# Loading x's second pair of tiles ahead of w_mod in an adaLN attention and gMLP kernel

## The chip, the cores and the metric

The kernel runs on one NeuronCore of a Trainium2 chip. The metric is device time in microseconds (us) of one execution, as the median of several runs. The core has five engines with one instruction list each: PE (matmul), ACT, DVE, POOL and SP; SP here only issues DMAs. An engine works through its list in order and stops at an instruction whose semaphores are not there yet.

## The reference, cut to what matters

The input is one sequence of 2048 positions with 448 channels; all arrays are bfloat16.

```python
mod = (silu(c) @ w_mod).reshape(1, 6, 1, 448)     # c: (1, 448), w_mod: (448, 6 * 448)
sa, ca, ga, sb, cb, gb = (mod[:, i] for i in range(6))
h = layernorm(x) * (1 + ca) + sa
x = x + ga * A(h)       # qkv, 16 heads of 28, causal window of 256, softmax, wo
h = layernorm(x) * (1 + cb) + sb
x = x + gb * B(h)       # gelu(h @ w_in), halves z1, z2; (z1 * (w_sp @ layernorm(z2) + b_sp)) @ w_out
```

## The kernel before, in words

Positions are cut into 16 tiles of 128, channels into 4 groups of 112 (CP) on the partitions. The work goes through these stages, which overlap.

**Head.** c is loaded as one row (L397) and turned onto partitions by four products with a one-element `one` (L520), each with a filler product beside it; silu writes sc_sb (L524). w_mod's first two of six parts (shift and scale) are loaded into wmodA in four pieces (L415), by part and by half of the contraction, on SP and ACT. t_mA (L548 to L555) multiplies wmodA's columns, 112 at a time, with silu(c); the moving operand is one column of sc_sb repeated 112 times, so that the result lies on partitions. DVE copies it to modT (L579, L580). x's first four tiles come in two pairs: load_x0(0) first, load_x0(1) behind w_mod and half of wk (L413 to L421). Layer norm statistics run on DVE (L632, L635, L637) with a power on POOL (L639), the normalization writes xn (L650 on DVE, or L655 and L657). The first four tiles are turned by PE (L746) and modulated while they are copied out of PSUM (L755 on ACT, L757 on DVE) into hT. Later tiles are turned by SP's transposing DMAs (L467) and modulated in hT (L736, L738).

wk and wq land in wq_st and are copied with padding into WQK (L621, L622). K (L827), Q (L803 for the first four tiles, L769 for the others) and V (L847) are then projected tile by tile and copied out of PSUM to KT, qT and Vaug (L839, L840, L808, L809, L778, L779, L851, L852). QBD holds copies of qT's parts (L797, L822 and others). Fillers are products of a constant tile with itself (`busy`, L517), which give PE work while it has none.

**Attention.** For each of 16 tiles and two halves of the heads: scores (L932, L962, L973), exponential on ACT (L918), causal and window mask on DVE (L981, L1002), product with V (L1009), division (L1023, L1025), a transposing DMA of o_sb, the product with wo (L1035) and the addition to x (L1039), the second layer norm and its transposing DMA. gg_sb (L601) holds the gates ga and gb, with which POOL scales wo (L605) and w_out (L1051).

**gMLP.** z1 and z2 (L1150, L1129) with gelu on ACT, the product with w_sp (L1174), z1 times it (L1178, L1181), w_out (L1193), addition to x (L1203), stores (L1208). w_sp is loaded by transposing DMAs on SP.

**What sets the order.** Every piece of work is an `Op` with the engines that could run it and an estimate of its duration. The string PLAN lists all ops, one word each: the engine's letter (p, a, d, t for POOL, s), the op's number, and the PSUM bank or buffer that it takes. It was searched ahead of time against the estimates, with `prio`, `land` (when a load is due) and `after` (an order between ops) as its guides, and is fixed in the file. `Sched.order` deals the words out to the engines' lists, `Sched.waits` finds the semaphore waits, `Sched.emit` writes the instructions. So PLAN alone decides on which engine a movable op runs, and where in that engine's list.

Of the kernel before, what the change touches and what calls it, by code (L numbers as in the profile page):

```python
# [5 lines left out]
BF16 = mybir.dt.bfloat16  # L6
# [6 lines left out]
d24 d22 p50.3 p52.1 p55.0 p46.1 p57.0 p54.3 a0 a3 d23 p37.0.1 p71.0 p63.3 p69.1 p73.0 p74.1 p61.0 p62.3 p60.2 s1  # L13
s2 d108 d110 s4 s6 s10 s8 s12 a5 a7 a9 a38 a39 p75.1 t27 t28 t29 t32 t33 t30 t31 a100 a106 d111 d109 t112 t113
t26 p42.1 p43 p58.3 p48.1 p44.0 p45 d114.3 d115.1 p124.6 p77.2 p64.0 p51.3 d83 p127.0 p70.1 p66.0 p72.2 p67.3
p65.0 p78.1 d82 d125 d128 t101 p139.1 t25 t102 p56.0 d126 p81.3 p76.1 p47.0 p80.3 p59.2 p53.1 p49.2 a105 t103
d129 p140 a141 a40 p148.5 p149 a150 d116 d118 d117 d119 d176 d180 d182 d178 d177 d183 d181 d179 t104 t107
p145.6 p146 a147 p136.1 p137 a138 s11 p151.5 p152 a153 p79.2 t120 t121 d123.0 d122.1 p130.7 p133.0 a134 d41
d131 t184 t185 d186.3 p68.0 p372.0 a373.2 p142.6 p143 a144 d132 d135 p154.7 p170.1 p171 p155 p378.0 s13 d241
d247 d245 s14 d308 d242 d156 d246 s15 s193 t187 t188.1 s194 p163.0 p164 t189 t190.2 s195 t191 t192.0 s196  # L20
a379.4 p397.0 t34 t35 d248 t36 d243 d382 d312 d306 d380 d309 d374 d376 p173.6 a172 p157.1 p158 p160.7 p174
a398.1 a165 p90.0 p91 d92 a399 p404.0 d402 d310 d244 d400 d169 p161 p93.0 t85 t84 a175 a159 p86.1 p87 d88 d89
p375.0 p377 p94 a405.3 a406 p425.0 p381 p383 a197 d199 t200 d198 p210.1 p211 t249 t250 t252 t253.2 t254 d95
p217.0 p218 s16 s19 a426.0.0 p433.0 d384 d385.1 p401.0 s386 a166 d407 p403 p408 a212 p204.1 p205 d311 d219
p201.0 p202 d409 s259 t255.1 d307 d313 t314 d167 d168 s260 d251.0 t256 s258 t257.3 s261 t315 t321 t319 t99 t98
t96 t97 a434.2 p453.0 d429 d203 d436 a206 p207.1 p208 p410 d411 d209 d430 d412.2 s413 d435 a162 p427.0 p220.0
p221 a454.1.1 p461.0 p229.1 p230 d457 a428 a222 p226.0 p227 d228 p431.0 p432 a462.6 p481.0 d463 a231 a482.4.2
s852 s17 s18 p437 p438 d439 d215 d440.1 s441 p223.0 p224 a225 p232.1 d458 d216 d213 d464 p489.0 a490.2 d492
p233 p235.0 p236 a237 p459.0 p455.0 p508.0 p414.0 p415 d416 t262 t264 t263 t265 a234 p387.1 p388 d389 d486
a456 p460 p465 p466 d467 d468.0 d485 t320.1 s325 t322.2 s469 s326 s21 a214 p483.0 p272.0 p273 a509.0.0 p536.0  # L30
p269.1 p270 d491 p487.0 a484 p510.0 p488 p493 a537.5.1 p516.0 d274 d316.0 s323 t317 t318.3 p494 d390 d391 t392
t393 d512 d513 d495 d496.1 s497 d394.1 t395 s324 t330 t327 t329 a271 a511 p266.1 p267 p538.0 p275.0 p276
a517.6 d519 d518 d417 p564.0 a268 p442.1 a277 p282.0 p443 p514.0 d444 d281 p515 p283 a565.4.2 d569 p544.0 d418
d445 t419 d278 p291.1 p520 p521 d522 d446 d540 d447 d541 a539 p292 a284 p288.0 p289 t448 t449 s396 t450.0 t328
t451 s20 s848 d523.1 s524 a545.2 p572.0 d546 d547 d568 a293 p294.1 p295 a290 p238.0 p239 p542.0 p543 p548
a573.0 d574 p592.0 p549 d550 d551.0 s552 s846 a240 p470.0 p471 p566.0 a296 p285.1 p286 d472 d279 a593.3.0
p600.0 p300.0 d575 d473 d596 d280 p570.0 p301 d302 a567 p571 p576 a601.2 p619.0 d602 p577 d597 d578 d579.1
s580 a287 p525.1 p337.0 p338 d474 p526 d527 a620.4.1 p627.0 d624 d623 d603 p594.0 a339 p553.0 p554 d555 p340.1
p598.0 p341 a628.5 p647.0 d475 d630 a595 p599 p604 d556 p605 d606 d607.0 s608 s452 t476 t477 t478.2 t420 t421
t422.1 d557 t423 t479 s480 s424 t558 t559 t560 a342 p498.1 p499 p621.0 d500 p297.0 p298 a648.6.2 p675.0 d629  # L40
d651 a622 p649.0 p625.0 p331.1 p332 a299 p334.0 p626 a676.3.0 p655.0 d501 d502 t503 d333 d652 d528 d679 p631
p632 p335 d633 d336 d344 a650 p347.1 p677.0 p348 a656.4 d657 p683.0 a678 a349 p609.0 p610 d611 d658 d680
d634.2 s635 a684.5 p359.1 p360 a361 p350.0 p351 a352 d612 d343 d613 d346 d345 p703.0 a704.2.1 d707 t504 d505.0
d686 t561.1 t562 t822 t614 t615 p353.1 p354 a355 p303.0 p304 a305 p653.0 p711.0 p654 p659 p660 d661 d662.1
s663 p356.1 p705.0 p581.0 p582 a712.1 p730.0 d685 d583 d713 d708 p681.0 p682 p687 p688 d689 d690.2 d714 a706
a731.0.2 d735 d734 p732.0 a733 t821 s563 s691 s853 s847 t506 s507 d529 t530 p357 d358 p738.0 a739.5 p365.0
p709.0 p710 p715 p366 a367 p716 d717 d584 d718.1 s719 t531 t532 t533.1 d585 t586 t824 t823 t534 t587 t588
t589.2 d740 d741 p758.0 a759.1.1 d763 p760.0 p362.0 p363 a364 a761 p664.1 p665 d666 d762 p736.0 p766.0 a767.3
# [12 lines left out]
t915 p945 a953 d955 d973 d954 d972 d941 d948 d949 d956 t950 d974 d896 t951 t957 t958 a836 a835 p1038.0 p1039.1
# [191 lines left out]
def bass_adaLN_cond__sliding_block__mixer_gmlp__prompt_kernel(  # L253
# [257 lines left out]


    hC = Hold(bM)
    hCW = Hold(bL)

    def busy(h):
        return lambda e: e.matmul(  # L517
# [57 lines left out]
    for op in fillers[30:]:  # L575
        op.deps.update(t_mA)
# [699 lines left out]
```

## Time and profile before

| what | us |
|---|---|
| median of 3 runs | 277.72 |
| the 3 runs | 277.67 to 277.77 |
| the profiled execution | 277.95 |
| its span, first to last instruction | 276.2 |
| busy in the span: PE, PEld (weight loads) | 268.6, 154.3 |
| busy in the span: DVE, ACT, POOL | 163.6, 124.1, 132.3 |

Between the first and the last instruction lies the span; the time of an execution is some 1.75 us longer. A busy engine in this profile is one with an instruction in flight, and the ends of matmuls are modelled. Idle time is put down to the instruction whose semaphore came last. Line numbers (L827) are those of the kernel before; in the changed file most stand one to four lines earlier (L1174 is L1173 there, L827 is L826).

### The profile page before, as it was taken

The numbers are of one execution on the slowest core, as the hardware profiler recorded it, in microseconds if no ns is written. First come the engines' busy times: TensorE is split into PE (matmuls) and PEld (weight loads), VectorE is DVE, ScalarE is ACT, GpSimd is POOL, SyncE is SP. The second block draws the span as 40 slices with busy tenths as digits, with TensorE's granted clock in tenths as the row PEclk, the third lists the DMA queues.
The fourth block names the chain that finished last, engine by engine and source line by source line (L and its number), as shares of the span: only waits on it lengthen the run. The fifth ranks groups of instructions, "written<-read, shape, count | busy, mean of one in ns | idle before, by whom it ended". The sixth has DMA issues, their size and how long they took to land.

```text
span 276.2 us, 8436 instructions
## 1 busy us (share of the span) xinstructions
PE 268.6 (97%) x3745; PEld 154.3 (56%) x3755; DVE 163.6 (59%) x365; ACT 124.1 (45%) x146; POOL 132.3 (48%) x190
## 2 busy tenths in 40 slices
PE   8989999999999999999999999999999999999995
PEld 5966677687667766454444444444444444445452
DVE  3599999999998999968979310014302213121454
ACT  3489899998889887365885500000000000000000
POOL 7563899438086285667567003316643303241400
PEclk9999999999999999999999999999999999999999
DMA  7999448578232497578599996000000001000114
GB/s 204 263 309 183 80 82 194 101 70 135 38 62 40 44 136 167 105 117 134 115 173 156 209 187 119 0 1 0 2 0 0 17 2 33 0 0 2 33 50 133
DMA packets 67302, 25.55 MB, mean 92 GB/s; under 512 B 58497, under 2 KB 66178, under 8 KB 67266
## 3 DMA queue, kind: packets, MB, share of 16 engines
q1 hardware_dynamic: 66304, 24.21, 46.8%
q10 hardware_dynamic: 962, 0.80, 1.1%
q8 instruction: 29, 0.48, 0.7%
q14 instruction: 7, 0.06, 0.1%
HBM read 9.01 MB, written 1.84 MB: 39 GB/s over the span
## 4 chain that ended last, share of the span: by engine, by line
PE 85%; ACT 4%; DVE 4%; DMA 3%; SPq 1%; issue 1%; POOL 1%; DVEq 0%
PE ps L1174 35%; PE ps L1129 8%; PE ps L1150 8%; PE ps L1193 8%; PE ps L962 5%; PE ps L1009 5%; ACT PW L918 4%; PE ps L1035 4%; PE ps L769 4%; PE ps L827 3%; DMA x_sb<-in_A_x_dram 3%; PE ps L847 3%; DVE PT L981 1%; PE ps L973 1%; DVE st_all L632 1%
## 5 line engine op out<-in xcount | busy, mean ns | idle before, releaser
L1181 POOL TENSOR_TENSOR z1T<-tmpg,z1T 128x512 bf16<-128x512 bf16 x28 | 32.1, 1153 | 75.3 <-DVE tmpg L1178 75.3
L918 ACT ACTIVATE PW<-ps 128x2048 bf16<-128x2048 f32 (+1 forms) x42 | 59.7, 1450 | 7.4 <-PE ps L962 6.8
L1178 DVE TENSOR_TENSOR tmpg<-ps,bsp_bc 128x512 bf16<-128x512 f32 x28 | 19.0, 689 | 72.9 <-PE ps L1174 68.1
L1174 PE MATMUL ps<-wspB,z 128*128 128x512 bf16 x218 | 49.0, 379 | 0.3
L1174 PE MATMUL ps<-wspA,z 128*128 128x512 bf16 x220 | 48.6, 379 | 0.3 <-issue 0.2
L981 DVE TENSOR_TENSOR PT<-PW,mask 128x1024 bf16<-128x1024 bf16 x56 | 40.6, 751 | 0.6 <-ACT PW L918 0.4
L1174 PEld LDWEIGHTS ps<-wspA,z 128*128 128x128 bf16 x224 | 21.8, 98 | 26.6 <-issue 0.4
L1174 PEld LDWEIGHTS ps<-wspB,z 128*128 128x128 bf16 x224 | 21.9, 98 | 26.3
L639 POOL TENSOR_TENSOR rs_all<-ve_all,neghalf 128x1 f32<-128x1 f32 (+2 forms) x37 | 24.6, 678 | 14.2 <-DVE ve_all L637 9.7
L1009 PE MATMUL ps<-Vaug,PT 128*128 128x32 bf16 x496 | 23.9, 177 | 0.0
L1009 PEld LDWEIGHTS ps<-Vaug,PT 128*128 128x128 bf16 x496 | 21.5, 96 | 2.3 <-issue 0.4
L1129 PE MATMUL ps<-w_in,hT 64*128 64x448 bf16 x224 | 22.2, 349 | 0.1
L1150 PE MATMUL ps<-hT,w_in 64*128 64x512 bf16 x196 | 22.2, 376 | 0.0
L1193 PE MATMUL ps<-w_out_g,z1T 128*128 128x448 bf16 (+2 forms) x119 | 22.0, 341 | 0.0
L632 DVE BATCH_NORM_STATS2 st_all<-x_sb 128x6 f32<-128x448 bf16 x32 | 18.8, 613 | 3.6 <-DMA x_sb<-in_A_x_dram 3.5
L1203 DVE TENSOR_TENSOR fin<-ps,x_sb 128x448 bf16<-128x448 f32 (+2 forms) x17 | 9.7, 594 | 18.5 <-PE ps L1193 17.0
L1009 PE MATMUL ps<-Vaug,PW 128*128 128x32 bf16 x224 | 20.2, 176 | 0.3 <-issue 0.3
L632 DVE BATCH_NORM_STATS2 st_all<-z 128x6 f32<-128x448 bf16 x32 | 18.8, 609 | 1.8 <-ACT z L1136 1.8
L657 POOL TENSOR_SCALAR xn<-x_sb,rs_all,ve_all 128x448 bf16<-128x448 bf16 x20 | 17.4, 869 | 3.4 <-DMA hT<-xn 2.1
L1158 ACT ACTIVATE z1T<-ps 128x512 bf16<-128x512 f32 x28 | 14.7, 601 | 9.2 <-PE ps L1150 9.1
L1009 PEld LDWEIGHTS ps<-Vaug,PW 128*128 128x128 bf16 x224 | 17.7, 96 | 1.8 <-issue 0.4
L962 PEld LDWEIGHTS ps<-qT,KT 32*128 32x128 bf16 (+1 forms) x1344 | 13.4, 90 | 8.7 <-ACT PW L918 6.1
(103 smaller groups left out, 368.6 us busy)
## 6 DMA issues: line engine op xcount, KB each, us to landing
out_dram<-fin SPq DMA_DIRECT2D x15, 112.0 KB, 1.7
wmodB<-in_w_mod_dram SPq DMA_DIRECT2D x1, 1568.0 KB, 14.1
x_sb<-in_A_x_dram SPq DMA_DIRECT2D x3, 448.0 KB, 9.8
w_in<-in_B_w_in_dram SPq DMA_DIRECT2D x3, 448.0 KB, 5.8
w_out_g<-in_B_w_out_dram SPq DMA_DIRECT2D x1, 784.0 KB, 5.1
bsp_bc<-in_B_b_sp_dram SPq DMA_DIRECT2D x1, 512.0 KB, 5.7
x_sb<-in_A_x_dram SPq DMA_DIRECT2D x2, 224.0 KB, 5.1
hT<-xn SPq DMA_TRANSPOSE x28, 3.5
```

The source lines that it names most:

```text
L632: st = [dve(0.62 if True else 0, lambda e, t=t, ci=ci, s=s: e.bn_stats(st_all[:, slot, t, ci, :], s()), deps(t), prio) for ci, s in enumer ...
L639: return pool(0.4 + 0.15 * len(tiles), lambda e: e.tensor_tensor(rs_all[:, slot, a:b], ve_all[:, slot, a:b], neghalf[:, 0:b - a], ALU.pow) ...
L918: ex = act(xdur, lambda e, out_ap=out_ap, in_ap=in_ap: e.activation(out_ap(), in_ap(), ACT.Exp, scale=SCALE), [s] + list(after), v - 8.0 + ...
L962: fm.append(lambda e, hm=hm, qi=qi, key=key, kn=kn, lo=lo, hi=hi, col=col, p0=p0, t=t, j=j: e.matmul(ps[p0:p0 + kn, hm.slot[t], col:col + ...
L981: return lock_d(0.68, lambda e: e.tensor_tensor(cols(hp.slot[0] * 2048 + 1024 * k, [[256, 4], [128, 2], [1, 128]]), cols(at_w() + pad + at ...
L1009: fns.append(lambda e, hp=hp, hO=hO, hi=hi, bi=bi, kb=kb, hd=hd, nb=nb, a=at[hi][bi], p_of=p_of: e.matmul(ps[:, hO.slot[0], 32 * hd:32 * h ...
L1129: return lambda e, kc, p0, start, stop: e.matmul(ps[:, hs[t % 2].slot[hf], 0:D], lhsT=hT[p0:p0 + 64, kc, t * 128:(t + 1) * 128], rhs=w_in[ ...
L1150: return lambda e, kc, p0, start, stop: e.matmul(ps[:, hs[b // 2].slot[b % 2], :], lhsT=w_in[p0:p0 + 64, kc, ft * 128:(ft + 1) * 128], rhs ...
L1174: m = pe(16 * MMS, [lambda e, h=h, si=si, ft=ft, tb=tb: e.matmul(ps[:, h.slot[0], :], lhsT=z2[:, si, ft * 128:(ft + 1) * 128], rhs=(wspA i ...
L1178: a = dve(0.7, lambda e, h=h, ht=ht, tb=tb: e.tensor_tensor(tmpg[:, ht.slot[0], :], ps[:, h.slot[0], :], bsp_bc[:, tb * 512:(tb + 1) * 512 ...
L1181: u = pool(1.16, lambda e, ht=ht, ft=ft, tb=tb: e.tensor_tensor(z1T[tb][:, ft, :], tmpg[:, ht.slot[0], :], z1T[tb][:, ft, :], ALU.mult), [ ...
L1193: return [lambda e, ft=ft: e.matmul(ps[:, h.slot[0], 0:hi - lo], lhsT=z1T[t // 4][:, ft, (t % 4) * 128:(t % 4 + 1) * 128], rhs=w_out_g[:, ...
```

## The change

Four things change beside the order of all ops. PLAN is replaced as a whole by another one found by the same kind of search; the ops and their estimates are the same except for those below. The core of the diff:

```diff
-    c_row, _, _ = alloc("c_row", [1, D], BF16)
-    one, _, _ = alloc("one", [1, 2], BF16)
+    c_row, _, _ = alloc("c_row", [128, D], BF16)
...
-    t_c = load("d_c", "act", 0.01, lambda e: e.dma_start(c_row[:], c[0:1, :]), prio=-98.97, land=2.5)
+    t_cz = add({"pool": (0.2, lambda e: e.memset(c_row[0:127, :], 0.0))}, (), -99.5)
+    t_c = load("d_c", "act", 0.01, lambda e: e.dma_start(c_row[127:128, :], c[0:1, :]), prio=-98.97, land=2.5)
...
-    t_wmA = [x for v in range(2) for x in load4("d_wmA%d" % v, wmodA, w_mod, slice(v * D, v * D + D), slice(v * D, v * D + D), -98.95, ((5.4, 4.9), (6.6, 6.3))[v])]
-    t_wk = load4("d_wk", wq_st, A_wqkv, slice(D, 2 * D), slice(D, 2 * D), -98.9, (8.4, 7.9))
-    t_wq = load4("d_wq", wq_st, A_wqkv, slice(0, D), slice(0, D), -98.8, (10.4, 9.3))
-    t_x0.append(load_x0(1, "sp", -98.85, 9.6))
-    for row in (t_x0[:1] + t_wmA[::2] + t_wk[:1] + t_x0[1:] + t_wq[:1], [t_c] + t_wmA[1::2] + t_wk[1:] + t_wq[1:]):
+    t_wmA = load4("d_wmA", wmodA, w_mod, slice(0, 2 * D), slice(0, 2 * D), -98.95, (6.9, 7.3), ("act", "sp"))
+    t_wk = load4("d_wk", wq_st, A_wqkv, slice(D, 2 * D), slice(D, 2 * D), -98.9, (8.3, 8.7), ("act", "sp"))
+    t_wq = load4("d_wq", wq_st, A_wqkv, slice(0, D), slice(0, D), -98.8, (9.8, 10.2), ("act", "sp"))
+    t_x0.append(load_x0(1, "sp", -98.97, 5.0))
+    for row in (t_x0 + t_wmA[1:] + t_wk[1:] + t_wq[1:], [t_c] + t_wmA[:1] + t_wk[:1] + t_wq[:1]):
...
-    t_cT = pe(1.32, [fn for ch in range(DC) for fn in (busy(hCW), lambda e, ch=ch: e.matmul(
-        ps[0:CP, hC.slot[0], ch:ch + 1], lhsT=c_row[:, ch * CP:(ch + 1) * CP], rhs=one[:, 0:1], start=True, stop=True))],
-        [t_c, t_p1, t_fill], -91.0, [hC, hCW])
+    t_cT = pe(0.22, [lambda e, ch=ch: e.matmul(
+        ps[0:min(128, D - ch * CP), hC.slot[0], 64 * ch:64 * ch + 64], lhsT=c_row[:, ch * CP:min(D, ch * CP + 128)], rhs=fill[:, 0:64], start=True, stop=True)
+        for ch in range(DC)], [t_c, t_cz, t_fill], -91.0, [hC])
...
-        v, kp = n // 2, n % 2
-        t_mA.append(pe(0.45, [lambda e, v=v, ch=ch, kc=kc: e.matmul(
-            ps[0:CP, hA[v].slot[0], ch * CP:(ch + 1) * CP], lhsT=wmodA[0:CP, kc, v * D + ch * CP:v * D + (ch + 1) * CP],
-            rhs=sc_sb[0:CP, kc:kc + 1].broadcast_to([CP, CP]), start=(kc == 0 and ch == 0), stop=(kc == DC - 1 and ch == DC - 1))
+        kp, v = n // 2, n % 2
+        wide = lambda ch, v=v: CP if v * D + ch * CP + 128 > 2 * D else 128
+        t_mA.append(pe(0.45, [lambda e, v=v, ch=ch, kc=kc, m=wide(ch): e.matmul(
+            ps[0:m, hA[v].slot[0], 64 * ch:64 * ch + 64], lhsT=wmodA[0:CP, kc, v * D + ch * CP:v * D + ch * CP + m],
+            rhs=sc_sb[0:CP, kc:kc + 1].broadcast_to([CP, 64]), start=(kc == 0 and ch == 0), stop=(kc == DC - 1 and ch == DC - 1))
...
-            [t_wmA[n], t_sc] + t_mA, -60.0, [] if kp else [hA[v]]))
+            [t_wmA[kp], t_sc] + t_mA, -60.0, [] if kp else [hA[v]]))
...
-    warm(30, 0.22, 900.0)
-    warm(6, 0.12, 901.0)
+    warm(27, 0.22, -99.0)
+    warm(4, 0.12, -59.0)
```

- **x.** SP issues both pairs of x's first tiles, then its half of w_mod, wk and wq; ACT issues c, then the other halves.
- **w_mod.** wmodA comes in two pieces instead of four, by halves of the contraction, with rows of 896 elements instead of 448. Each product group of t_mA needs one of the two pieces.
- **c.** c_row has 128 rows, 127 of them zeroed by POOL, and c in the last. Four products with 64 columns of ones turn it; the four fillers between are gone.
- **Modulation.** The weights are 128 columns wide (112 at the end of the array), of which 112 rows of the result are used; the moving operand is 64 columns wide.
- **Fillers.** 31 instead of 36 (and the four named), placed: nine ahead of c's products, 18 up to the modulation, four after it.
- **Order.** In the new PLAN the first four tiles are modulated five times by DVE and three times by ACT (seven and one before), three of the eight WQK copies are on DVE (none before), and up to the last mask of attention DVE has two more copies to KT, three more to qT, three more modulations of hT, two of the four scalings of wo, two more normalizations, and six fewer copies to QBD, which ACT has. On SP the third group of x's transposes stands ahead of the first transpose of o_sb, and w_mod's last four parts are loaded ahead of x's last four tiles.

151 lines of the change are left out of this document (75 added, 76 removed).

## The prediction

> **What bounds the kernel now.** I read the busy times by stretches first, then the chain of work that ended last, then the first 20 us in order of time. The stretches give span:length, then busy time (and count) of PE, PEld, DVE, ACT and POOL, then granted clock, DMA share and GB/s.
>
> ```profile
> 0.00:18.24 18.24, 16.26 (x172) 12.31 (x173) 10.19 (x35) 9.48 (x14) 11.26 (x26) 1.00 0.97 253
> 18.24:111.47 93.23, 91.36 (x2578) 66.08 (x2579) 87.79 (x182) 84.08 (x86) 58.59 (x82) 1.00 0.65 109
> 111.47:155.20 43.73, 43.60 (x444) 20.83 (x443) 37.18 (x105) 28.08 (x43) 27.41 (x53) 1.00 0.82 138
> 155.20:273.20 118.00, 117.37 (x557) 55.08 (x565) 27.79 (x45) 2.47 (x5) 35.02 (x31) 1.00 0.17 37
> ```
>
> From 111 us on PE idles 0.13 and 0.63 us, and the change reorders products there but alters none; after 273.2 come one addition and one store, as before. That part stays, unless attention hands over late. The stretch to 111.47, mostly attention, is tight on three engines: PE idles 1.87 us, DVE 5.44, ACT 9.15. What is loose is the head (start, length, engine, line, work):
>
> ```profile
> 11.20 1.50 PE L827 MATMUL ps<-hT,WQK 112*128 112x128 bf16 x24
> 12.55 1.95 PE L803 MATMUL ps<-hT,WQK 112*128 112x128 bf16 x32
> 14.51 0.92 PE L847 MATMUL ps<-wv,hT 112*128 112x448 bf16 x4
> 15.26 0.27 PE L517 MATMUL ps<-fill 128*128 128x256 bf16 x1
> 15.95 0.65 PE L746 MATMUL ps<-ident,xn 128*112 128x128 bf16 x8 [0.41 <-DVE xn L650]
> 16.44 0.27 PE L517 MATMUL ps<-fill 128*128 128x256 bf16 x1
> 16.64 0.29 PE L932 MATMUL ps<-qT,KT 32*128 32x128 bf16 x8
> 16.87 0.93 PE L847 MATMUL ps<-wv,hT 112*128 112x448 bf16 x4
> 18.24 0.23 PE L803 MATMUL ps<-hT,WQK 112*128 112x128 bf16 x1 [0.45 <-DVE hT L757]
> ```
> ```profile
> 22.45 0.89 PE ps L827 x16
> 23.34 0.76 PE ps L847 x4
> ```
>
> The K and Q products of the first two tiles run from 11.20; the second pair of x tiles is normalized so late that PE turns it only at 15.95 and projects it at 18.24. By the chain's pitches (second fence: 16 K products 0.89, a V group 0.76) the work from 11.20 to 18.24 is 24 + 32 products (3.1), two V groups (1.5), a score group (0.3) and eight turns (0.4): 5.3 of 7.0 us. The other 1.7 are fillers and waits.
>
> **The change in the head.** Loads first (KB, then us from issue to landing), and SP's issues:
>
> ```profile
> x_sb<-in_A_x_dram SPq DMA_DIRECT2D x1, 224.0 KB, 7.5
> wq_st<-in_A_wqkv_dram ACTq DMA_DIRECT2D x1, 196.0 KB, 6.8
> wq_st<-in_A_wqkv_dram SPq DMA_DIRECT2D x1, 196.0 KB, 7.6
> ```
> ```profile
> wmodA<-in_w_mod_dram SPq DMA_DIRECT2D x1, 196.0 KB, 5.3
> ```
> ```profile
> 1.32 0.94 SPq L406 DMA_DIRECT2D wmodA<-in_w_mod_dram  x2
> 2.31 0.47 SPq L406 DMA_DIRECT2D wq_st<-in_A_wqkv_dram  x1
> 2.82 0.47 SPq L410 DMA_DIRECT2D x_sb<-in_A_x_dram  x1
> 3.33 0.53 SPq L406 DMA_DIRECT2D wq_st<-in_A_wqkv_dram  x1
> ```
> ```profile
> 3.47 1.15 DVE L632 BATCH_NORM_STATS2 st_all<-x_sb 128x6 f32<-128x448 bf16 x2 [2.40 <-DMA x_sb<-in_A_x_dram]
> ...
> 8.60 0.16 DVE L580 TENSOR_SCALAR modT<-ps 112x4 f32<-112x4 f32 x1 [1.80 <-PE ps L551]
> 8.67 0.15 DVE L579 COPY modT<-ps 112x4 f32<-112x4 f32 x1
> 8.90 1.52 DVE L757 TENSOR_SCALAR hT<-ps,modT 112x256 bf16<-112x256 bf16 x4
> ```
>
> x's first pair lands at 3.5 (DVE's wait ends), w_mod's last piece at 1.8 + 5.3 = 7.1, the second pair at 2.8 + 7.5 = 10.3, wq's last at 3.3 + 7.6 = 10.9. So 1,792 KB (x 224, w_mod 784, wk and wq 784) land from 3.5 to 10.9: 240 KB/us over both queues. Now SP issues both x pairs and then its half of w_mod, ACT issues c and the other half. At half the rate the second pair lands at 3.5 + 224/120 = 5.3. SP's half of w_mod lands at 7.7 if only x and w_mod go before it (1,008 KB behind the first pair), at 8.5 if ACT's wk shares the way (196 more). No byte is saved, so wq still ends near 10.9; what wider rows may save I count as nothing.
>
> The modulation products go from 112 to 128 weight columns and from 112 to 64 moving columns. Today 1.5 us pass from w_mod's landing to modT (8.60); half of that may go, and I take 0.7 for the third of four product groups to come through: 8.4, 9.2 at the late landing. Turning c takes four products for eight; silu stands 3 us ahead of w_mod's landing either way, so nothing. The memset of c_row on POOL is of the size of POOL's other small memsets, well under 1 us, ahead of work that is waited for only at 5; without that cover it would delay the first normalization, which now has over 1 us to spare.
>
> In DVE's new order come the second pair's statistics (5.3 to 6.5), aggregates and the first pair's normalizations, modT's shift (waits for three product groups), the second pair's two normalizations (I take 0.4 each, as a turn: 1.52/4), and only then modT's scale: 9.4, or 10.2, against 8.76 now. Behind that wait queues the whole turn of the first pair. It then runs on two engines, DVE (a turn, a WQK copy, a turn: 1.2) beside ACT (two turns), so K's large group starts at 10.7 to 11.5, against 11.20. Q waits for three more turns and two WQK copies on DVE (2.0): 12.6 to 13.4, against 12.55. I take 12.8: the second pair is turned by then, Q ends at 14.6, the first scores at 14.9. Against the state of before at 18.24 two V groups are missing (1.5): 16.4. **Lead of the head: 1.8 us**; 2.0 to 1.2 by w_mod's landing.
>
> **The change in the order.** Counted over both streams, PE's products are the same but for those above. What moves is work from POOL to DVE and ACT. Prices (the number before the second bar is ns of one):
>
> ```profile
> L797 DVE COPY QBD<-qT 32x512 bf16<-32x512 bf16 x11 | 4.8, 434 | 0.3
> ...
> L840 DVE CAST KT<-ps 128x512 bf16<-128x512 f32 x2 | 1.4, 692 | 0.3 <-PE ps L827 0.2
> L601 DVE COPY gg_sb<-ps 128x448 f32<-128x448 f32 x2 | 1.2, 616 | 0.0
> L852 DVE CAST Vaug<-ps 128x448 bf16<-128x448 f32 x2 | 1.2, 603 | 0.0
> L738 DVE TENSOR_SCALAR hT<-hT,modT 112x512 bf16<-112x512 bf16 x2 | 1.1, 613 | 0.0
> L822 DVE COPY QBD<-qT 32x256 bf16<-32x256 bf16 x3 | 0.9, 287 | 0.1
> L662 DVE COPY xn<-xn 128x64 bf16<-128x64 bf16 x4 | 0.7, 178 | 0.1
> ```
> ```profile
> L981 DVE TENSOR_TENSOR PT<-PW,mask 128x1024 bf16<-128x1024 bf16 x56 | 40.6, 751 | 0.6 <-ACT PW L918 0.4
> ```
> ```profile
> L981 DVE TENSOR_TENSOR PT<-PW,mask x56: 654/684/1525, 32.9 to 110.4; 128x1024 bf16<-128x1024 bf16 x56
> ```
> ```profile
> DVE rec_all L1023 <- PE ps L1009: 2.1, 6, 0.5
> DVE x_sb L1039 <- PE ps L1035: 1.9, 3, 0.9
> ```
>
> Up to the last mask DVE gains two KT and three qT copies (0.69 each, 3.5), three hT modulations (1.8), two scalings of wo (0.62 as L601, 1.2), two normalizations (0.8), three WQK copies and one of wmodE (not shown on DVE; between 0.29 as L822 and 0.69 as L840, I take 0.4: 1.6) and eight small ones (0.18 each, 1.4). It loses six QBD copies to ACT (2.6), two turns (0.8), a statistic and an addition (1.2). In all +5.7 us, from 5.3 to 6.9 with the unknown ones. Relief comes from POOL: masks have a median of 684 ns and a mean of 751, the excess being those that meet POOL's work; POOL gives up what DVE gains in SBUF (hT, wo, normalizations, wmodE, small ones: 5.6 us at DVE's prices, a tenth of its 58.6), so of 56 x 0.067 = 3.8 I take 0.4, the ends being 0 and 3.8.
>
> DVE's last mask ends at 111.47, after 8.05 us of idle in the head (first fence) and 5.4 from there on: 98.0 of work. Changed: 98.0 + 5.7 - 0.4 = 103.3, plus an idle head of some 5 by the walk above: the last mask ends at 108.3 + x, x being DVE's idle time behind the head. To keep the whole lead it must end at 111.47 - 1.8 = 109.7, so x = 1.4. Most of today's 5.4 is waiting for PE (last fence, 4.0), which shrinks when PE is ahead; 1.4 remain. I take x = 2.0, so 0.6 of the lead is eaten and **1.2 us** stay.
>
> ACT gets some 0.8 us more (six QBD copies for KT, qT and WQK copies) and starts its exponentials about 2 us sooner; its 9.15 idle hides that, and without it 0.8 would be lost. On SP the first two transposes of o_sb stand behind x's third group now; the product that reads them is put off by four tiles anyway, so nothing; were it not, each would cost what it waits. One load of w_in and some pieces of w_sp move back in SP's list as well; w_sp's first reader starts at 155.2, with a list that ends with them. After attention DVE has 2 us more and 6.5 idle there.
>
> **Sum.** The profiled execution took 277.95 (span 276.2, 1.75 around it); less 1.2 it is 276.75. The median shown, 277.72, is 0.23 below that execution, so the forecast is **276.5**.
>
> **Rivals.**
>
> - *No change, 277.5.* The pair isn't ahead in effect: both queues share the rate, ACT's w_mod rows are twice as wide as x's, and if an engine alternates between them by rows, x gets a third, 80 KB/us: its second pair lands at 3.5 + 224/80 = 6.3 and w_mod's end at the late 8.5 or behind. The lead is then 1.2 at most, DVE's head idles 0.6 longer, and with x = 2.4 the last mask ends at 108.9 + 2.4 = 111.3: 0.2 stays. For it: x's first load shares its way already. Against: 6.3 still precedes w_mod. [...]
> - *Slower, 279.9: DVE becomes the bound of attention.* Place: the masks L981. If DVE idles as now, x = 5.4, the last mask ends at 113.7, 2.2 late, and the last P.V products and all behind them as well: 277.72 + 2.2. It decides from x = 3.7 (over 0.55 lost). For it: 5.7 us more on an engine with 5.4 to spare. Against: its waits are mostly for PE.
> - *More, 275.0.* The lead stays whole (1.8) and half of PE's 1.87 idle in attention goes too, since exponentials are further ahead (0.9). Against: these waits lie at many places.
>
> **Chances and range.** Forecast (276.0 to 277.1) 0.42, more 0.18, no change 0.20, slower 0.20. A measurement of this kernel tells 0.2% (0.55 us) from none: faster 0.60, same 0.20, slower 0.20. The range takes in the third rival and most of the second: 274.5 to 279.2.
>
> **What would show it.** x's second pair landed by 5.3 to 6.3; modT's scale near 9.5; K's large group near 10.9, Q's first near 12.8, first scores by 15.2. In attention, DVE idle of 1.5 to 2.5 us from there to the last mask, and that mask done near 110.3; the first spatial product near 154.0 (155.2 now). I am wrong if the first scores come after 16 (the head), or come early while the last mask still ends at 111 or later (DVE), or if PE's stretch behind attention grows.

## The result, and the profile after

The changed kernel takes 289.34 us (median of 4 runs, 286.51 to 290.59), the kernel before beside it 277.75; the ratio is 1.0393 (95% interval 1.031 to 1.0475). It is slower by 11.6 us; the forecast was 276.5. The ratios, here and below, leave out single executions that lie more than 1.5% above the fastest of their kernel (at most three of twelve); the medians keep them. The profiled execution of the changed kernel took 290.59 us (span 288.5), that of before 277.95 (276.2).

Three moments cut both executions in the same way: the first scores, the end of the last mask, the first spatial product (the product with w_sp). Behind the last of them the two agree: 276.2 - 155.23 = 288.5 - 167.47 = 121.0 us.

| us | first scores | last mask ends | first spatial product |
|---|---|---|---|
| before | 16.64 | 111.47 | 155.23 |
| changed | 15.16 | 118.25 | 167.47 |

The head did what was forecast. The next fence is the changed kernel in order of time (start, length, engine, line, in brackets the idle time and what ended it).

```profile
5.96 1.15 DVE L631 BATCH_NORM_STATS2 st_all<-x_sb 128x6 f32<-128x448 bf16 x2 [0.96 <-DMA x_sb<-in_A_x_dram]
...
10.28 0.15 DVE L579 TENSOR_SCALAR modT<-ps 112x4 f32<-112x4 f32 x1
...
11.14 2.15 PE L826 MATMUL ps<-hT,WQK 112*128 112x128 bf16 x32
...
13.28 1.95 PE L802 MATMUL ps<-hT,WQK 112*128 112x128 bf16 x32
15.16 0.29 PE L931 MATMUL ps<-qT,KT 32*128 32x128 bf16 x8
```

x's second pair is there at 5.96, and the first scores come 1.48 us ahead of 16.64. All that is lost is lost between 15.16 and 167.47: 152.31 us for 138.59, 13.7 more. The page of the profile shows where; the first row is PE's busy tenths in 40 slices, the second its granted clock, the third the granted clock in the kernel before.

```profile
PE   8798999769999998899899999999999999999995
PEclk9999999959999999599999999999999999999999
```
```profile
PEclk9999999999999999999999999999999999999999
```

There are two holes, stretches in which PE waits, each with a halved clock behind it, where before every digit of the clock was a 9. The busy times by stretches measure them (span:length, then PE, PEld, DVE, ACT, POOL busy with counts, then the granted clock, DMA share, GB/s).

```profile
18.24:54.00 35.76, 34.41 (x911) 24.17 (x910) 34.56 (x78) 32.95 (x36) 17.25 (x24) 1.00 0.87 118
54.00:60.40 6.40, 1.60 (x59) 0.80 (x56) 0.83 (x4) 2.83 (x3) 0.00 (x0) 0.79 1.35 122
60.40:64.50 4.10, 4.08 (x48) 2.04 (x52) 2.92 (x6) 0.63 (x1) 0.00 (x0) 0.50 0.27 52
64.50:112.00 47.50, 46.68 (x1401) 34.41 (x1390) 44.18 (x97) 43.89 (x44) 17.58 (x28) 1.00 0.44 68
112.00:117.00 5.00, 2.92 (x103) 2.14 (x104) 4.06 (x10) 2.98 (x3) 2.91 (x4) 0.87 0.61 108
117.00:122.40 5.40, 5.40 (x51) 2.62 (x48) 1.98 (x5) 1.36 (x2) 3.38 (x7) 0.50 0.37 74
122.40:167.47 45.07, 43.73 (x439) 20.65 (x435) 39.14 (x107) 28.65 (x44) 25.91 (x52) 1.00 0.90 162
```

In the first hole PE works 1.60 of 6.40 us (4.8 lost), then 4.1 us at clock 0.50, in which half is lost (2.0): 6.8 us. In the second it is idle for 2.1 us, then works 5.4 us at 0.50 (2.7 lost) and a part of the five before them: about 5. In the last stretch PE idles 1.3 us. Together this is some 13 of the 13.7.

What ended the first hole stands in SP's list. SP's issues in order of time:

```profile
40.55 5.12 SPq L467 DMA_TRANSPOSE hT<-o_sb  x2
45.72 1.91 SPq L434 DMA_DIRECT2D w_in<-in_B_w_in_dram  x2
47.67 0.48 SPq L436 DMA_DIRECT2D w_in<-in_B_w_in_dram  x1
48.19 6.16 SPq L467 DMA_TRANSPOSE wspA<-in_B_w_sp_dram  x2
54.40 1.99 SPq L467 DMA_TRANSPOSE hT<-o_sb  x1
```

and the waits it caused, from the view of waits (us, times, longest) and in order of time:

```profile
DVE o_sb L1024 <- DMA hT<-o_sb: 5.6, 1, 5.6
PE ps L1034 <- DMA hT<-o_sb: 3.1, 1, 3.1
```
```profile
50.60 0.92 PE L1034 MATMUL ps<-wo_g,hT 112*128 112x448 bf16 x4
...
56.70 0.61 PE L961 MATMUL ps<-qT,KT 32*128 32x128 bf16 x48 [1.71 <-issue]
60.42 1.65 PE L1034 MATMUL ps<-wo_g,hT 112*128 112x448 bf16 x4 [3.10 <-DMA hT<-o_sb]
```

The transpose issued at 54.40 is that of o_sb's second tile, which DVE wrote from 38.27 to 38.87. The first row of the fence with SP's issues holds the transposes of the first and of the *third* tile: the second was put behind the third, which DVE writes until 44.46 and SP issues at 44.49, and behind 1.1 MB of w_in and a pair of w_sp's transposing loads. That pair keeps SP 6.2 us. The tile lands 5.9 us after its issue (median of the 16 transposes of o_sb in the kernel: 3.5). PE has reached its reader, L1034, 3.1 us earlier, and DVE cannot write o_sb's fifth tile, for o_sb has three buffers and the second is still being read. The same four products take 0.92 us at 50.60 and 1.65 at 60.42: that is the halved clock. Of the 1.71 us ahead of 56.70 the profile names no cause. One candidate stands in the trace: a load of instructions (16 KB, queue q8) that takes 1.1 us at 45.64 and 1.5 at 57.73 took 3.1 us there, from 52.24 to 55.32; that PE waited for it is not shown.

The second hole has two waits, and the first of them is not one for a transpose:

```profile
113.92 0.19 PE L1008 MATMUL ps<-Vaug,PT 128*128 128x32 bf16 x1 [1.31 <-DVE x_sb L1038]
...
116.70 2.05 PE L1128 MATMUL ps<-w_in,hT 64*128 64x448 bf16 x10 [0.78 <-POOL hT L1059]
```

1.31 of the 2.1 us end with DVE's addition to x, and the clock fell at 115.7, ahead of the wait for hT.

### The profile page after: what moved, and what is told of

It reads as the page before. It is cut to its first block, busy times and chain, and to the rows that moved or that the text cites. A ratio compares the mean times of both kernels' runs of the same rounds, so it can differ in the third digit from the quotient of the medians.

```text
span 288.5 us, 8424 instructions
## 1 busy us (share of the span) xinstructions
PE 272.5 (94%) x3746; PEld 154.6 (54%) x3746; DVE 166.9 (58%) x381; ACT 125.4 (43%) x148; POOL 113.7 (39%) x172
## 4 chain that ended last, share of the span: by engine, by line
PE 57%; DVE 19%; DMA 9%; ACT 7%; SPq 4%; POOL 2%; issue 1%; DVEq 0%; ACTq 0%
PE ps L1173 34%; PE ps L1192 7%; ACT PW L917 5%; DVE st_all L631 4%; DMA hT<-xn 4%; PE ps L1128 4%; PE ps L1149 3%; DVE PT L980 3%; SPq L467 3%; DMA wmodA<-in_w_mod_dram 2%; PE ps L961 2%; PE ps L1034 2%; DMA hT<-o_sb 2%; PE ps L1008 2%; DVE o_sb L1024 1%
## 5 line engine op out<-in xcount | busy, mean ns | idle before, releaser
L1173 PE MATMUL ps<-wspB,z 128*128 128x512 bf16 x224 | 49.6, 379 | 0.0
L980 DVE TENSOR_TENSOR PT<-PW,mask 128x1024 bf16<-128x1024 bf16 x56 | 37.8, 701 | 1.4 <-ACT PW L917 1.4
L638 POOL TENSOR_TENSOR rs_all<-ve_all,neghalf 128x1 f32<-128x1 f32 (+2 forms) x37 | 25.5, 698 | 4.3 <-DVE ve_all L636 2.8
L1128 PE MATMUL ps<-w_in,hT 64*128 64x448 bf16 x224 | 24.7, 371 | 0.8 <-POOL hT L1059 0.8
L1034 PE MATMUL ps<-wo_g,hT 112*128 112x448 bf16 x64 | 16.9, 386 | 3.3 <-DMA hT<-o_sb 3.1
L961 PE MATMUL ps<-qT,KT 32*128 32x128 bf16 (+5 forms) x1344 | 17.3, 198 | 2.4 <-issue 1.7
L1135 ACT ACTIVATE z<-ps 128x896 bf16<-128x896 f32 x16 | 14.0, 919 | 11.7 <-PE ps L1128 6.9
L737 POOL TENSOR_SCALAR hT<-hT,modT 112x512 bf16<-112x512 bf16 x7 | 6.0, 871 | 32.3 <-DMA hT<-xn 32.3
```

Source lines behind the costliest of these rows:

```text
L638: return pool(0.4 + 0.15 * len(tiles), lambda e: e.tensor_tensor(rs_all[:, slot, a:b], ve_all[:, slot, a:b], neghalf[:, 0:b - a], ALU.pow) ...
L961: fm.append(lambda e, hm=hm, qi=qi, key=key, kn=kn, lo=lo, hi=hi, col=col, p0=p0, t=t, j=j: e.matmul(ps[p0:p0 + kn, hm.slot[t], col:col + ...
L980: return lock_d(0.68, lambda e: e.tensor_tensor(cols(hp.slot[0] * 2048 + 1024 * k, [[256, 4], [128, 2], [1, 128]]), cols(at_w() + pad + at ...
L1034: mo = pe2(4 * MMD, [lambda e, h=h, j=j, ch=ch: e.matmul(ps[:, h.slot[0], 0:D], lhsT=hT[0:CP, ch, j * 128:(j + 1) * 128], rhs=wo_g[0:CP, c ...
L1128: return lambda e, kc, p0, start, stop: e.matmul(ps[:, hs[t % 2].slot[hf], 0:D], lhsT=hT[p0:p0 + 64, kc, t * 128:(t + 1) * 128], rhs=w_in[ ...
L1173: m = pe(16 * MMS, [lambda e, h=h, si=si, ft=ft, tb=tb: e.matmul(ps[:, h.slot[0], :], lhsT=z2[:, si, ft * 128:(ft + 1) * 128], rhs=(wspA i ...
```

## The experiments

The runs stood beside the kernel before on the same chips, where its median was 277.91 to 279.56 us. In the diffs a word of PLAN is an engine's letter and an op's number. s843 and s846 are the pair of w_sp, s18, s17 and s19 the loads of w_in between the transposes, s16 w_in's last load, s406 and s434 the transposes of o_sb's second and third tile, s364 and s830 the loads of w_out and b_sp, s832 one of w_sp's transposing loads. Dots in a diff stand for words left out.

**The pair of w_sp moved.**

```diff
-p529.0 ... p480.0 s19 s843 s846 p537.0
+p529.0 ... p480.0 s19 p537.0
...
-... p463.1 s318 d321
+... p463.1 s318 s843 s846 d321
```

> The changed kernel with two of SP's instructions moved: the pair of transposing loads of w_sp that stand between the loads of w_in and the third transpose of o_sb go back behind the next group of x's, where SP stands idle. Queue theory: in the changed kernel SP spends 48.2 to 54.4 us on this pair, with three loads of w_in (1.1 MB) in flight, and the third tile of o_sb, written at 50.7 us, is only issued at 54.4 and lands at 60.3; the stall of PE at 55 to 60 us (5.4 us idle, then 4 us of products at half clock, so some 7 us) goes: 289.3 less 7, 282 us (281 to 284), and the clock's dip near 58 us is gone. Bandwidth theory: the loads of w_in hold the transposes up whatever stands ahead of them; the tile lands before 58 us by the shorter queue but late, and under 2 us are won: 287.5 to 289. Order theory (the engines' own lists, DVE's above all): nothing changes, 288.5 to 290.

284.56 us (ratio to before 1.0183, 1.0123 to 1.0243), 0.6 above the range of the queue theory and far under the other two. The first hole and its clock are gone: the transpose is issued at 47.98, the reader runs at 56.38, the last mask ends at 112.85. The expectation took 50.7 us for the time at which the tile is written; that is another tile, and this one had been waiting since 38.9.

**The loads of w_in moved.**

```diff
-... t90 s18 d478 ... a261 s17 d484 ... p480.0 s19 s843 s846
+... t90 d478 ... a261 d484 ... p480.0 s843 s846
...
-... p696.0 s844 s601
+... p696.0 s844 s18 s17 s19 s601
```

> The changed kernel with three others of SP's instructions moved: the three loads of w_in (1.1 MB) that stand ahead of that pair go back to about 82 us, where SP and the DMA engines have room; the pair of w_sp stays ahead of the third o_sb. Queue theory: without the loads in flight the pair takes SP 1.3 us each, as single ones do elsewhere, so SP is free at 48.4 us, before the tile of o_sb is written (50.7 us): the stall goes as in the run without the pair, 282 us (281 to 284). So each move alone is enough; they do not add. Bandwidth theory: all of it goes here and little in the run without the pair. Order theory: 288.5 to 290.

283.12 us (1.015, 1.0093 to 1.0207). The pair keeps SP 2.76 us now for 6.16, the transpose is issued at 48.60, the reader runs at 55.55. Either move is enough, as the queue theory has it. The order theory is out, and so is the bandwidth theory, by which the first of the two moves wins little.

**The transpose moved, and no load.** Either move also takes bytes away from the transpose's way. This run leaves every load where it was.

```diff
-t256 t258 s379 s434 p268.0
+t256 t258 s379 s406 s434 p268.0
...
-p278.1 ... p279 s406 t315.0
+p278.1 ... p279 t315.0
```

> The changed kernel with one instruction of SP moved and no load: the transpose of o_sb's second tile, which the change put behind the third tile's transpose, two and a half loads of w_in and the pair of w_sp (it is issued at 54.4 us; DVE wrote its tile near 38.3 us), goes ahead of the third tile's. It is then issued near 41.8 us. Theory of the place in the list: the first stall goes as when loads were moved (284.6 and 283.1 us), 283 to 285, though every byte is in flight at the time it was. Theory of the bytes: the loads in flight hold up other transposes as well, the next ones (x's at 54 to 56 us) become the late ones, and under 2 us are won: 287.5 to 289.5.

284.83 us (1.022, 1.017 to 1.0271). SP's issues:

```profile
39.69 5.39 SPq L467 DMA_TRANSPOSE hT<-o_sb  x3
45.12 2.23 SPq L434 DMA_DIRECT2D w_in<-in_B_w_in_dram  x2
47.39 0.48 SPq L436 DMA_DIRECT2D w_in<-in_B_w_in_dram  x1
47.92 4.17 SPq L467 DMA_TRANSPOSE wspA<-in_B_w_sp_dram  x2
52.13 3.36 SPq L467 DMA_TRANSPOSE hT<-xn  x2
```

All three transposes of o_sb are out before the loads, the second tile's reader runs at 55.00, and from 50 to 68 us PE has no wait over 0.71 us. The place of one instruction in SP's list was worth 4.5 us. The bytes in flight are not enough to make the hole; they lengthen the time for which SP is kept (4.17 us for the pair here, 6.16 in the changed kernel, 2.76 with w_in's loads gone).

**The same place in the kernel before.**

```diff
-d430 d412.2 s413 d435
+d430 d412.2 s413 s441 s17 s18 s21 s852 s848 d435
```
(Numbers of the kernel before: s441 is the transpose of o_sb's third tile, s17, s18 and s21 are loads of w_in, s852 and s848 the pair of w_sp. All six are taken out at their old places.)

> The kernel before with nothing changed but SP's list: its two loads of w_in, a half load and the pair of w_sp stand together behind the third transpose of o_sb and ahead of the next transposes of x and o_sb, as in the changed kernel. Queue theory: SP is held from 44 to 53 us, the transposes due at 47.1 and 49.2 us land 6 to 8 us late, PE waits 3 to 6 us for them and its products then run at half clock for some us: 282 us (280 to 285), with a dip of the clock in the slices of 50 to 65 us. Rival: the old lists leave the transposes so much room that it costs nothing, and the changed kernel's stall needs its own tighter lists: 277.5 to 278.5.

278.68 us (0.9998, 0.9967 to 1.003): nothing. My theory missed here, and its rival held. SP is kept for 6.4 us (44.64 to 51.08) where the changed kernel has 8.7 (45.72 to 54.40),

```profile
46.34 4.70 SPq L467 DMA_TRANSPOSE wspA<-in_B_w_sp_dram  x2
51.08 1.28 SPq L467 DMA_TRANSPOSE hT<-xn  x1
52.40 2.16 SPq L467 DMA_TRANSPOSE hT<-o_sb  x1
```

and the transpose that goes out at 52.40 instead of 49.22 is that of the fourth tile, whose product PE reaches at 64.50 us in the kernel before and at 65.36 here. In the old lists the tile behind the loads is read 13 us after its issue; in the new ones it is due 3 us after it. Being 3.2 us late cost nothing here (ratio 0.9998); in the changed kernel, where the room to the reader was used up, PE waited 3.1 us.

**The last load of w_in moved.** The wait for hT in the second hole begins the same way:

```profile
108.13 0.58 SPq L434 DMA_DIRECT2D w_in<-in_B_w_in_dram  x1
108.75 1.20 SPq L467 DMA_TRANSPOSE hT<-xn  x1
```

The chain of waits of the changed kernel goes on from there: the transpose, POOL's modulation, PE's first products of w_in.

```profile
108.75 5.24 DMA hT<-xn
114.00 0.09 issue
114.09 2.40 POOL hT L1059 x3
116.48 0.21 issue
116.70 4.29 PE ps L1128 x22
```
```diff
-p735 ... d607 s16 p686
+p735 ... d607 p686
...
-... p696.0 s844 s601
+... p696.0 s844 s16 s601
```

> The changed kernel with one load moved: the last 448 KB of w_in, which SP issues at 108.1 us just ahead of a transpose of the next stage's hT that then takes 5.2 us (3.6 is the median), goes forward to about 82 us. Queue theory: the second stall (112 to 122 us: 2.1 us idle, then 6.0 us of products at half clock, 5.1 us in all) becomes shorter by the 1.5 us that the transpose is late and, as no window of idle PE then halves the clock, by up to 5: 285 us (284 to 288). The first stall stays. Rival: the second stall is the tail of the first one, whose 7 us shift every engine against the transposes; the load has nothing to do with it and 288.5 to 290 come out.

286.88 us (1.0279, 1.0192 to 1.0366). It lies in the range of the queue theory, but the gain of 2.5 us is not clear of the noise, for the interval overlaps that of the changed kernel (1.031 to 1.0475). POOL's wait for that transpose falls from 4.1 to 2.0 us and PE's only from 0.8 to 0.7, and another hole opens: PE waits 3.5 us at 130.8 to 134.3 for hT. That w_in's last load causes the second hole is thus not shown.

**All six moved.** Diff: the three moves above together.

> The changed kernel with all six of these moved (the pair of w_sp, the three loads of w_in, the last load of w_in). Queue theory: both stalls go, 12 us less: 277 us (275.5 to 278.5), and if the start's lead (first scores 1.5 us earlier) is kept as well, below the kernel before. Rival, stalls that belong to the engines' lists: 285 or more.

283.61 us (1.0162, 1.0108 to 1.0217); 277 was expected and 285 by the rival, so both missed. It is no better than the move of w_in's three loads alone (283.12). The attention is good now: first scores at 14.87, last mask at 110.80. But from there to the first spatial product pass 49.6 us for 43.8, and PE meets one more wait, on a transpose behind loads:

```profile
PE ps L1149 <- DVE hT L1059: 2.1, 1, 2.1
```
```profile
113.78 1.52 SPq L1081 DMA_DIRECT2D bsp_bc<-in_B_b_sp_dram  x1
115.35 1.19 SPq L467 DMA_TRANSPOSE wspA<-in_B_w_sp_dram  x1
116.58 1.26 SPq L467 DMA_TRANSPOSE hT<-o_sb  x1
117.89 0.58 SPq L866 DMA_DIRECT2D w_out_g<-in_B_w_out_dram  x1
118.51 7.22 SPq L467 DMA_TRANSPOSE hT<-xn  x4
```

**These loads moved as well.**

```diff
-... s500 s584 t635 a1013 s830 s832 d636 ... s795 a818 s364 d717
+... s500 s584 s364 t635 a1013 d636 ... s795 a818 d717
...
-... s667 d720.2 ... s838 d1001
+... s667 s832 d720.2 ... s838 s830 d1001
```

> The changed kernel with all six of the first moves (its first stall is gone then, attention's last mask ends at 110.8 us for 111.5 before the change, yet 49.6 us pass from there to the first spatial product for 43.8), and three more of SP's instructions moved: the load of w_out (784 KB) from 117.9 to some 113.8 us, b_sp's (512 KB) from 113.8 to some 150 us, one of w_sp's behind the four transposes of the next stage's x. Queue theory: those four stand at 118.5 us right behind 1.3 MB of loads, the first lands after 5.3 us, PE waits 2.1 us at 127 to 129 us and runs at half clock for some 3.5 us: with the loads away they are issued 1.5 to 2 us sooner and land in 3 us, PE waits under 0.5 us and keeps its clock: 280.0 us (279 to 281.5) for 283.6. Rival: the lists of DVE, ScalarE and GpSimd are what makes hT late (statistics, xn, then the transposes), and the loads' place is worth less than 1 us: 282.8 to 284.

283.11 us (1.0156, 1.0107 to 1.0205), where 280.0 was expected; it lies in the range of the rival. PE's wait of 2.1 us for hT is gone (two others for hT remain, 1.7 us together), but the moved piece of w_sp is now late itself (PE waits 1.7 us for w_sp at the first spatial product), and the profiled execution began with a halved clock (0.50 from 10 to 12 us): its first scores came at 16.47.

**Fillers in the start's wait, and w_sp's piece put back.** Two runs have this edit. The first has all the moves above but that of s832; the second has none of them: it is the change's start up to the gates with the old lists behind it, which the next part introduces (216 words).

```diff
-    def warm(n, dur, prio):
+    def warm(n, dur, prio, k=1):
...
-            fillers.append(pe(dur, [busy(hW)], [t_fill], prio, [hW]))
+            fillers.append(pe(dur, [busy(hW)] * k, [t_fill], prio, [hW]))
...
-    warm(4, 0.12, -59.0)
+    warm(4, 0.12, -59.0, 3)
...
-p41.1 p42 ... p71.2 p72.2 p73.2
+p41.1 p71.2 p72.2 p73.2 p42
```

> The changed kernel with its six loads and pieces moved, w_out's load four us sooner, b_sp's some 35 us later (the piece of w_sp that was moved with them stays: behind its move the first spatial product waited 1.7 us for w_sp), and the nine fillers in the wait of the start. Queue theory: 280.5 us (279.5 to 281.5), with no slice of a lowered clock: the rest over the kernel before, some 2.5 us, is products left over behind the last mask (PE works 45 to 47 us there for 43.6). Rival, that the new lists hold a wait of their own behind the attention that the loads' places don't touch: 282 to 284.

281.56 us (1.0123, 1.0074 to 1.0171), 7.8 us under the changed kernel, just above the 279.5 to 281.5 expected and under the rival's 282. The profiled execution, 279.80, has no slice with a lowered clock; two of the six have a mean clock of 0.992 and 0.994 and lie at 283.6 and 283.2. Its stretches around the last mask:

```profile
18.24:110.61 92.37, 89.21 (x2519) 63.79 (x2516) 87.51 (x192) 84.36 (x87) 40.33 (x57) 1.00 0.64 98
110.61:156.69 46.08, 44.89 (x464) 21.62 (x461) 40.03 (x109) 29.03 (x45) 27.30 (x56) 1.00 0.91 163
```

The mask ends 0.9 us sooner than before, and the stretch behind it takes 2.3 more (46.08 for 43.76): 1.3 of products left over, 1.1 of idle. In the idle PE waits 0.9 us for hT and 0.8 for w_sp.

> The run of the start and the gates with the old lists, and three of the start's fillers moved: PE waits 1.2 to 1.7 us there between the two halves of the modulation's products for SP's half of w_mod, and in one profile the granted clock fell to 0.50 behind that wait (10 to 12 us) and the first scores came at 16.5 us instead of 14.7. Nine filler products now stand in that wait. Theory that the clock at the start is a gamble: five of the other run's twelve executions, those with a mean clock under 0.996, lie at 280.3 to 283.9 us, the rest at 278.0 to 280.0; with the fillers all executions are of the second kind, median 278.7 us (278.0 to 279.3), ratio 0.999 to 1.003. Theory that the spread comes from elsewhere (DMA): median stays at 279.5 to 280.5. In either case the lead of 1.9 us at the first scores gives nothing at the end, as DVE's last mask came at 111.5 us in all versions with the old lists: not under 277.5.

280.42 us (1.0073, 1.0041 to 1.0104): a miss. In the profiled execution w_mod was later still, PE waited through the fillers, and the clock fell:

```profile
10.00:12.00 2.00, 1.82 (x23) 1.53 (x22) 1.89 (x7) 1.03 (x2) 1.25 (x3) 0.75 1.12 283
12.00:14.00 2.00, 2.00 (x22) 2.00 (x20) 1.17 (x5) 0.86 (x2) 0.60 (x2) 0.50 1.14 233
```

First scores 16.74. Nine fillers were too few for this wait; that more of them would hold the clock wasn't tried. Nor does the clock account for the median: three of the twelve executions have a mean clock under 0.996, and the other nine still lie at 278.8 to 281.5 us.

**The start alone, with the old lists behind it.**

```diff
-PLAN = the words of the change
+PLAN = their first 164, then all other ops as the kernel before has them
```

> The change's start alone: its loads, its turn of c, its modulation by 128 columns, and its lists up to the first exponentials (the first 164 words of the plan); from there on every engine's list, and the engine of every instruction, is that of the kernel before. Theory: the start's lead is real (first scores 15.2 us for 16.6) and only the new lists behind it lose; the old lists keep it up to the last mask but for what DVE eats, so the forecast of the prediction holds here: 276.3 us (275.5 to 277.0), first spatial product at 153.8 us for 155.2. Rival: the lead is eaten in the attention by the tight engines whatever the lists, 277.5 (277.2 to 278.0). Second rival: the start's own edits cost something behind them (x's loads against w_k's), above 278.

279.23 us (1.0027, 0.9993 to 1.0061). The forecast of 276.3 is out, and by the ratio nothing is won, as the first rival has it; the median lies above 278, where the second has it. The first scores come at 14.61, 2.0 us ahead, and the last mask ends at 111.06, 0.4 ahead; behind it 1.0 us more is lost (44.78 us to the first spatial product for 43.76), 1.1 of it in one wait of L1030. Up to 30 us PE loses 2.4 of the lead at the gates' products:

```profile
PE ps L593 <- DVE gg_sb L596: 1.3, 1, 1.3
PE ps L593 <- ACT Vaug L846: 1.1, 1, 1.1
```

With 216 words of the change, the gates among them:

> The change's start with the old lists, taken over later than in the run of the start alone: the first 216 words of the plan are the changed kernel's (up to the modulation for the second stage and the gates, some 24 us), the rest is the kernel before. In the run of the start alone (279.2 us, ratio 1.003) the lead of 2.0 us at the first scores was gone by 30 us: PE waited 2.4 us at the gates' products for DVE's and ScalarE's copies, which in the old lists stand behind work that is not yet due. Theory that the lead was lost to this seam: with the gates where the changed kernel has them 276.8 us (276.0 to 277.7), 0.9935 to 0.998 of the kernel before. Theory that DVE and ScalarE, busy 13.9 and 11.3 of 15.4 us there, eat any lead: ratio 0.998 to 1.004.

280.11 us (1.0053, 1.0016 to 1.0091), above the ranges of both theories. These waits are gone, yet the last mask ends at 111.48, where it ended before. So the seam is not what costs the lead of 1.9 us. Another wait stands there instead, 1.6 us of PE for DVE's o_sb, and DVE works 88.98 of the 93.24 us from 18.24 on (87.79 of 93.23 before). That full engines eat the lead fits this, but no run shows it.

**DVE relieved.** In the run with the pair moved, 13 norm instructions go back to POOL:

```diff
-d193 d245 d246.0 d255 d312 d313.3 d321 d496 d416 d442 d472 d444 d607
+t193 t245 t246.0 t255 t312 t313.3 t321 t496 t416 t442 t472 t444 t607
```

> The changed kernel with the pair of w_sp moved, and with 13 instructions of the two layer norms in the attention, which the change moved from GpSimd to DVE, back on GpSimd, at the same places of the lists: DVE loses some 5 us of work up to its last mask. Theory that DVE bounds the attention: last mask 2 to 4 us earlier, 281 to 283 for 284.6. Theory that the late transposes and stalls bound it, and not DVE's amount of work: GpSimd does each of them two to three times slower, the transposes behind them start later, 284.5 to 287.

284.33 us (1.0205, 1.0158 to 1.0252), for 284.56. DVE works 84.69 us for 87.92 up to the last mask, which ends at 112.96 for 112.85. So taking 3.2 us of work from DVE wins nothing. As the same instructions take longer on POOL (L656, a normalization: 886 ns there and 481 on DVE in the changed kernel), this speaks against DVE's amount of work as the bound and does not rule it out.

**The old lists behind the new attention.**

```diff
-PLAN = the words of the change, the pair moved
+PLAN = their first 728, then all other ops as the kernel before has them
```

> The changed kernel with the pair of w_sp moved as in the run that took the first stall away (284.6 us there, first spatial product at 160.0 us), and with the lists of the kernel before from the last scores on (behind the first 728 words of the plan). Theory that the rest of the loss lies behind the attention, where products of the next stage wait 3.2 us for hT that lands late: 281 to 282. Theory that it lies in the attention, where DVE has 5.7 us more to do and its last mask ends at 112.9 us for 111.0: the products behind it only wait elsewhere, 284 to 285.

289.1 us (1.0355, 1.0294 to 1.0416): worse by 4.5, for PE waits 4.8 us for o_sb's transposes in two places. Both theories missed. It tells only that a tail fits the lists ahead of it.

No version here beats the kernel before.

## Why the prediction was wrong

**The step that failed** is the one on SP: "On SP the first two transposes of o_sb stand behind x's third group now; the product that reads them is put off by four tiles anyway, so nothing; were it not, each would cost what it waits. One load of w_in and some pieces of w_sp move back in SP's list as well". The room to the reader was real: tile written at 38.9, product due at 57.3. I did not put the moved loads into that room. Behind the third tile's issue (44.49 to 45.7), two and a half loads (2.4 us of SP), a pair of w_sp (6.2) and the landing (5.9) the tile is there at 60.3, 18 us of room used and 3 more. Priced at nothing, it costs 4.5 to 6.2 us by the medians of the three runs that undo it, or 4.8 to 6.7 us by their ratios to the kernel before beside them. That SP's time for an issue rises from 1.3 to over 3 us behind 1.1 MB was in no row that I had quoted.

**The clock** had no term. In the profile of the changed kernel each hole costs its idle time and then half of 4 to 5 us of products: 2.0 and 2.7 us. Not every hole does: behind the 3.5 us at 130.8 to 134.3, in the run with w_in's last load moved, the clock stayed at 1.00.

**"That part stays"** (the stretch behind the attention) failed with it: 49.2 us for 43.8. With the loads moved it is 46.1, so a part is of the same kind, transposes behind b_sp's and w_out's loads. Another part is not: the wait for DVE's addition at 113.92, and what is left of the 46.1 over 43.8. I had named the growth of this stretch as what would prove me wrong, and no price.

**The head** was right: second pair 5.96 (5.3 to 6.3 forecast), K's large group 11.1 (10.7 to 11.5), Q 13.28 (12.6 to 13.4), scores 15.16 (14.9). modT's scale came at 10.28, just past the late end (10.2), since SP's half of w_mod landed at 8.8 and not 7.7 to 8.5; the lead in the profiled execution is 1.5 us (1.8; 2.0 to 1.2). The rival in which both queues share the rate is not out in the head: it has the pair at 6.3 and w_mod at 8.5 or behind, which fits 5.96 and 8.8 as well as the forecast does. From 3.0 to 4.5 us SP's queue, with x's rows, moved 0.12 MB in 135 packets and ACT's, with w_mod's wider ones, 0.33 MB in 188, so x had less than the third that the rival gave it; from 4.5 to 5.1 it had over half. These packets are a row long (896 B of x, 1,792 of w_mod); whether an engine alternates by them stays open. Only the rival's lead, 1.2 at most, is too small for the measured 1.5.

**DVE's sum** was right by luck, through two errors that cancel. Forecast: 103.3 us of work, 5 of idle in the head and x = 2.0 behind it, last mask at 110.3; with all the loads moved and the fillers it ends at 110.6. In that run DVE's idle from 18.24 on is 92.37 - 87.51 = 4.9, and its work up to the mask is 99.2 us: against 98.0 + 5.7 the relief is some 4.5 us and not 0.4. The masks carry most of it; this row is the changed kernel's:

```profile
L980 DVE TENSOR_TENSOR PT<-PW,mask 128x1024 bf16<-128x1024 bf16 x56 | 37.8, 701 | 1.4 <-ACT PW L917 1.4
```

701 ns for 751, 56 of them: 2.8 us. I had taken a tenth of the bound of 3.8, and three quarters came, while POOL's work up to the mask fell from 69.9 to 49.9 us. In the kernel before the 15 masks that meet no work of POOL take 668 to 693 ns and the 41 that meet some 776 on average; in the changed kernel 26 of the 56 meet some. The rival in which DVE bounds the attention would have x = 4.9 end at 113 or later; it ends at 110.6, and the run that relieves DVE moved nothing. That rival's sign was right; for its mechanism nothing speaks. (The range I gave does not take in "most of" this rival either: it ends at 279.2, and the rival's time is 279.9.)

**The gain** at the mask, 0.9 us in the best case for the 1.2 forecast, isn't kept by the stretch behind it. Why 1.3 us more of products are left over there is open, and so are the 3.7 us by which the best version with the new lists stays behind the kernel before (281.56 for 277.91).

## What to carry to other kernels

When an order is changed, walk the DMA queue's own list like an engine's: for each transfer, what stands ahead of it, what the queue waits for there, and how far behind it its reader stands. In these runs a transfer late by less than that room cost nothing (3.2 us late and 13 of room: ratio 0.9998), and one late by more cost the excess (3.1 us of PE's wait), what queues behind the reader, and, where it fell, the clock behind the hole (2.0 us). Bulk loads whose readers come much later (w_in is loaded at 45.7 us here and first read at 116.7) belong where the queue is idle, not between two transposes that feed the next product.

## What the runs showed of the hardware

SP's time for a transposing issue isn't fixed: in the changed kernel ten of the sixteen of w_sp take 1.29 to 1.30 us, and the pair behind 1.1 MB of w_in takes 3.1 on average (6.16 for two). With w_in's loads moved away the same two take 2.76 us.

PE's granted clock in the changed kernel fell from 1.00 to 0.50 at 57.7 us, when PE had done 0.6 us of work since 55.0, and rose again at 64.5, after 4.1 us of work; it fell again at 115.7 and rose at 122.6. Both stretches at 0.50 are 6.83 us long, and the two falls lie 58.0 us apart. Eight other profiled executions have a mean clock of 0.994 or less. If all of that is lost at 0.50, the 0.994 of four of them comes to 3.4 us each (w_in's three loads moved, its last load moved, b_sp's and w_out's loads moved, the start with fillers), the 0.992 of three to 4.5 us, and in the run with the old lists behind the new attention the 0.90 from 114.21 to 166.42 us to some 10. What sets these lengths is not shown. In the 3.4 us ahead of the first fall of the changed kernel PE had worked 1.3 us, and in the 3.4 us ahead of the second 2.1. So the clock fell behind stretches in which PE was busy for over a third of the time, and what decides is open.

This also bears on the 3.5 us of idle at 130.8 to 134.3, in the run with w_in's last load moved, behind which the clock stayed at 1.00 (PE idles 4.7 us there from 112.09 to 163.79, and the clock of that stretch is 1.00). And it bears on the start: the clock fell there in two profiled executions of the new start, with PE waiting 1.7 us for w_mod (b_sp's and w_out's loads moved) and 1.5 us (the start with fillers), and stayed at 1.00 with a wait of 1.4 us in the changed kernel. From 6 to 10 us PE idles 1.7 and 1.5 us in those two; with all six loads and pieces moved it idles 2.2 us, and the clock stayed at 1.00. So the length of PE's idle time alone does not decide it.
